# A sliding-window attention with a highway layer: loads of the first blocks by another queue and in another layout, a first batch pair by query blocks, and the highway layer in pairs of token blocks

## The chip, the cores and the metric

The kernel runs on one core of a Trainium2 chip. The metric is the device time of one execution in microseconds. Five engines work side by side, each on its own queue of instructions in order: TensorE (PE, with its weight loads PEld), VectorE (DVE), ScalarE (ACT), GpSimd (POOL) and SyncE (SP). GpSimd and SyncE also issue the DMAs here.

## The reference, cut to what matters

```python
B, H, S, D = 8, 8, 576, 64
scores = q @ k.T / 8                        # per batch and head
rel = pos[:, None] - pos[None, :]
mask = (rel >= 0) & (rel < 128)             # 128 keys back at most
scores = where(mask, scores - slopes[h] * abs(rel), -1e9)
attn = softmax(scores)
x = concat_heads(attn @ v)                  # 4608 tokens x 512
H_ = maximum(x @ w_h, 0)
T_ = 1 / (1 + exp(-(x @ w_t + b_t)))
out = T_ * H_ + (1 - T_) * x                # fp32
```

## The kernel before, in words

**Tiling.** Two batches form a pair m (0 to 3); the two lie on the two halves of the 128 rows (64 dimensions each) when scores are computed. The 576 tokens are blocks 0 to 3 of 128 and a narrow block 4 of 64 (the tail, both batches together on 128 rows). A block of queries sees its own block of keys and the one before it.

**Loads.** GpSimd casts fp32 to bf16 while loading. `load_qk` (L98) brings q or k in pieces of four tokens (1 KB read in one piece); for pair 0 the first half of the rows comes in eight loads of four heads and one batch, the second half in two. `load_v` (L123) brings one block of v in pieces of one token and head (256 B read), `load_tails` (L115) the narrow block. w_h is loaded by SyncE in fp32 into the room of q of pair 1 and cast by ScalarE (L221, L227); w_t and the bias come by GpSimd (L230).

**Attention.** TensorE transposes q and k (L251), DVE or ACT copies them out of PSUM (L277). Keys and queries of a load in pieces of four stand in a permuted order, which the copies of k undo and the masks for q take up. Per head: scores (L304), exp on ACT with the key's part of the slope as bias (L337), the mask as a product on DVE for two heads (L352), the product with v that has a column of ones (L375, matmuls at L393), and the division by the sum (L399, L409 and L410) into x. A pair is worked in stages, which `STAGES` and `ORDER` (L43, L51) set: pair 0 in four of 256 columns (a to d: blocks of keys 0, 1, 2, 3), the others in two of 512 (A, B).

**Highway layer**, per block of 128 tokens (36 in all, each a group of its own, `GROUPS`, L56): four transposes of x (L433), a copy (L442), four matmuls with w_h (L449), relu less x on DVE (L456), four matmuls with w_t (L465) and one that adds the bias by a one-hot row (L467), tanh on ACT (L473), the step from tanh to the gate on GpSimd (L478; on DVE in the last blocks), gate product on DVE (L483), addition of x on GpSimd (L489; the last on DVE), and the store by SyncE in four DMAs (L505), two for a tail (L497).

**Order.** A planner's output is written out: `ISSUE` (L714) lists the nodes in the order in which they are issued, `BANKS` (L750) the PSUM bank of each tile (eight banks; a score tile or a product with v of four or more blocks takes two). Each engine runs its instructions in that order. The nodes (L592 to L709) name their dependences; the costs and due times beside them are the planner's input and have no effect when the kernel runs. Pools (L65) bound how many tiles are alive.

Of the kernel before, what the change touches and what calls it, by code (L numbers as in the profile page):

```python
# [10 lines left out]
P = 128  # L11
# [3 lines left out]
def kernel(  # L15
# [30 lines left out]
        "a": ((0, 0, 0), (0, 1, 128)),  # L46
        "b": ((1, 1, 0), (1, 2, 128)),
        "c": ((2, 2, 0), (2, 3, 128)),
        "d": ((3, 3, 0), (3, 4, 128), (4, 4, 192)),
    }  # L50
    ORDER = ("abcd", "AB", "AB", "AB")  # L51
    DMA_X = ()

    HOME = {"A": ("A", 0), "B": ("B", 0), "a": ("A", 0), "b": ("A", 256), "c": ("B", 0), "d": ("B", 256)}

    GROUPS = {  # L56
        "A": ((0,), (1,), (2,), (3,)), "B": ((0,), (1,), (2,), (3,), (4,)),
        "a": ((0,), (1,)), "b": ((0,), (1,)), "c": ((0,), (1,)), "d": ((0,), (1,), (2,)),
    }

    ADD_MASK = ()
# [36 lines left out]
    def load_qk(m, w, x=None, hs=None):  # L98
        src, dst = ((q, QL), (k, KL))[w]
        ps = slice(0, P) if x is None else slice(64 * x, 64 * x + 64)  # L100
        for r in (slice(0, 2),) if hs is None else (0, 1):
            hh = slice(0, H) if hs is None else slice(4 * hs, 4 * hs + 4)
            if hs is None:
                o = dst[m % 2][ps].rearrange("p r h n -> p (r h) n")
                i = src[2 * m : 2 * m + 2, :, 4 * ps.start : 4 * ps.stop, :].rearrange(
                    "r h (p t) d -> p (r h) (t d)", t=4
                )
            else:
                o = dst[m % 2][ps, r, hh, :]
                i = src[2 * m + r, hh, 4 * ps.start : 4 * ps.stop, :].rearrange(  # L110
                    "h (p t) d -> p h (t d)", t=4
                )
            nc.gpsimd.dma_start(out=o, in_=i)  # L113
# [22 lines left out]
    MKA = ADD_MASK and cp.tile([P, H, 2 * P], BF16, name="mka")  # L136
    cvec = cp.tile([P, H], F32, name="cvec")
    ones1 = cp.tile([P, P], BF16, name="ones1")
    wH = cp.tile([P, NCK, DM], BF16, name="wH")
# [25 lines left out]


    BIG = float(2**20)

    def c_mka():
        nc.vector.tensor_scalar(out=MKA[:, :, 0:P], in0=bc(tri[:, 0, :], P), scalar1=BIG,  # L170
                                scalar2=-BIG, op0=ALU.mult, op1=ALU.add)
        for h in range(H):
            nc.vector.tensor_scalar(
                out=MKA[:, h, P : 2 * P], in0=tri[:, 1, :], scalar1=BIG,
                scalar2=-BIG - P * slopes[h] / scale, op0=ALU.mult, op1=ALU.add,
            )

# [13 lines left out]
    def c_vec():  # L191
        nc.vector.memset(ones1[:], 0.0)
        nc.vector.memset(ones1[0:1, :], 1.0)
        nc.vector.memset(bT[:], 0.0)
        for h in range(H):
            nc.vector.memset(cvec[:, h : h + 1], float(np.exp(-float(P) * slopes[h])))
# [20 lines left out]

    def w_stage():
        return QL[1][:].rearrange("p r h n -> p (r h n)").bitcast(F32)

    def load_wf():  # L221
        nc.sync.dma_start(
            out=w_stage().rearrange("p (c n) -> p c n", c=NCK),
            in_=moe_w_h.rearrange("(c p) n -> p c n", p=P),
        )

    def cast_wf():  # L227
        nc.scalar.copy(out=wH[:].rearrange("p c n -> p (c n)"), in_=w_stage())

    def load_w(n):  # L230
        if n == 2:
            nc.gpsimd.dma_start(out=bT[0:1, :], in_=moe_b_t.rearrange("(o n) -> o n", o=1))
        else:
            nc.gpsimd.dma_start(
                out=(wH, wT)[n][:],
                in_=(moe_w_h, moe_w_t)[n].rearrange("(c p) n -> p c n", p=P),
            )
# [5 lines left out]
    def chunks(m):  # L243
        return (0, 1) if ORDER[m][0] == "a" else (None,)

    def tr_parts(m):

        ps = [(x, hs) for x in chunks(m) for hs in range(4 if x is None else 2)]
        return ps + ["tail"]

    def transposes(m, w, part):  # L251
# [11 lines left out]
        x, hs = part  # L263
        L = (QL, KL)[w][i]
# [12 lines left out]
    def evac(m, w, part):  # L277
# [7 lines left out]
        x, hs = part  # L285
        nh, n0, n = (2, 0, P) if x is None else (4, 64 * x, 64)
# [14 lines left out]
    def width(kind):  # L301
        return 512 if kind in "AB" else 256

    def scores(m, kind, h):  # L304
        i, W = m % 2, width(kind)
        if W == 512 or h % 2 == 0:
# [3 lines left out]
        sc, o = SC[m, kind, h], 0 if W == 512 else (h % 2) * W  # L310
        qm = QT[i][:, h, 0:512].rearrange("p (t c q) -> p c t q", t=4, c=4)
        segs, n, add = STAGES[kind], 0, m == 0 and kind in ADD_MASK
        if add and h % 2 == 0:
            for r in range(2):
                nc.tensor.matmul(
                    out=sc[:, r, :], lhsT=ident[:],
                    rhs=MKA[:, h : h + 2, :].rearrange("p h n -> p (h n)"),
                    start=True, stop=False,
                )
        while n < len(segs):  # L320
            j, qb, off = segs[n]
            two = n + 1 < len(segs) and segs[n + 1][0] == j and segs[n + 1][1] < 4
            for r in range(2):
# [3 lines left out]
                else:  # L327
# [4 lines left out]
                    rhs=rhs, start=not add,  # L332
                    stop=not add or (h % 2 == 1 and n + 1 + two >= len(segs)),
# [3 lines left out]
    def soft(m, kind, h):  # L337
        W, (home, c0) = width(kind), HOME[kind]
        if h % 2 == 0:
            if c0 == 0:  # L340
                PT[m, home, h // 2] = ptp[home].tile([P, 2, 2, 512], BF16, name="pt")
            for j, qb, off in STAGES[kind]:
                COL[m, h // 2, j, qb] = (PT[m, home, h // 2], c0 + off)
        o = 0 if W == 512 else (h % 2) * W
        nc.scalar.activation(  # L345
            out=PT[m, home, h // 2][:, h % 2, :, c0 : c0 + W],
# [5 lines left out]
    def mask(m, kind, g):  # L352
        home, c0 = HOME[kind]
        o = PT[m, home, g]
# [3 lines left out]
        else:  # L358
            rep, lo, W = 2, c0, width(kind)
            if kind == "b":  # L360
                lo = 0
# [53 lines left out]

    def grp(m, kind, gi):
        bs = GROUPS[kind][gi]
# [9 lines left out]
    def f_x(m, kind, gi):  # L427
# [3 lines left out]
        for i in range(n):  # L431
            for c in range(NCK):
                nc.tensor.transpose(  # L433
                    out=pt[:, c * P : (c + 1) * P], in_=x[:, i, c * P : (c + 1) * P],
# [3 lines left out]
    def f_xe(m, kind, gi):  # L438
# [4 lines left out]
            out=xt[:, 0:n].rearrange("p i c n -> p i (c n)"), in_=TR[m, kind, gi][:, 0:512].rearrange("p (i n) -> p i n", i=1)  # L443
        )

    def f_h(m, kind, gi, i):
        AH[m, kind, gi] = ps_tile(1)
        for c in range(NCK):
            nc.tensor.matmul(out=AH[m, kind, gi], lhsT=XT[m, kind, gi][:, i, c, :],  # L449
                             rhs=wH[:, c, :], start=c == 0, stop=c == NCK - 1)  # L450

    def f_u(m, kind, gi):
# [4 lines left out]
            out=uu[:, 0:n, :], in0=AH[m, kind, gi].rearrange("p (i n) -> p i n", i=1), scalar=0.0, in1=x,  # L457
            op0=ALU.max, op1=ALU.subtract,
        )

    def f_z(m, kind, gi, i):
        AZ[m, kind, gi] = ps_tile(1)
        az = AZ[m, kind, gi]
        for c in range(NCK):
            nc.tensor.matmul(out=az, lhsT=XT[m, kind, gi][:, i, c, :], rhs=wT[:, c, :],  # L465
                             start=c == 0, stop=False)
        nc.tensor.matmul(out=az, lhsT=ones1[:], rhs=bT[:], start=False, stop=True)  # L467

    def f_th(m, kind, gi):
# [3 lines left out]
        nc.scalar.activation(out=tt[:, 0:n, :], in_=AZ[m, kind, gi].rearrange("p (i n) -> p i n", i=1), func=ACTF.Tanh,  # L473
# [11 lines left out]
    def f_out(m, kind, gi, eng):  # L485
        bs, n, x = grp(m, kind, gi)
        ot = op.tile([P, 2, DM], F32, name="ot")
        OT[m, kind, gi] = ot
        eng.tensor_tensor(out=ot[:, 0:n, :], in0=UU.pop((m, kind, gi))[:, 0:n, :], in1=x, op=ALU.add)  # L489
# [302 lines left out]
```

The softmax here doesn't subtract the row's maximum and nothing guards it: scores larger than these inputs give would overflow.

## Time and profile before

| | |
|---|---|
| three runs | 175.17, 175.18, 175.36 us; median 175.18 |
| profiled execution | 175.22 us, of which the span 173.5 |
| granted TensorE clock | 0.987 |
| mean of one instruction | exp of 1024 columns 1119 ns, of 512 696; mask of 1024 753, of 2048 1454; relu less x 684; gate product 538; tanh 602; copy of x 589; POOL addition 1365 |
| largest waits of engines | POOL for the gate product 24.8 us, ACT for scores 13.2, ACT for the gate's matmuls 11.9, PE for k 7.9 |

A row of the page names line, engine, operation, out<-in and count, then busy time and mean of one instruction, then the engine's idle time before it and what ended that. A window row names the stretch, then busy time of PE, PEld, DVE, ACT and POOL. The chain is followed back from the last instruction to what released each step. In the slices a digit is the busy share in tenths. A busy PE has matmuls in flight, which is not the same as full speed.

### The profile page before, as it was taken

How to read it: one execution, taken by the hardware profiler on the slowest of the kernel's cores; microseconds unless marked ns; L12 is line 12 of the kernel's file. 1: busy time of each engine (PE TensorE's matmuls, PEld its weight loads, DVE VectorE, ACT ScalarE, POOL GpSimd, SP SyncE). 2: the span in 40 equal slices, each digit the busy share in tenths (PEclk: the TensorE clock that was granted, in tenths of full speed). 3: DMA queues.
4: the chain of work that ended last, by engine and by line, in shares of the span. 5: the costliest groups of instructions: out<-in, count | busy, mean ns of one | idle time of the engine just before them, and what ended most of it. 6: DMA issues, size and time to landing. Idle time of an engine off the chain costs nothing.

```text
span 173.5 us, 5255 instructions
## 1 busy us (share of the span) xinstructions
PE 150.3 (87%) x2132; PEld 92.8 (54%) x2132; DVE 140.0 (81%) x244; ACT 125.4 (72%) x178; POOL 118.1 (68%) x132
## 2 busy tenths in 40 slices
PE   0169789999799789999999979999999999999930
PEld 0158544666566347766556755566556556754410
DVE  5087686999898888999867999889887899976580
ACT  2625678797799969899779968799898897235510
POOL 7997373488883799984067985884485969676540
PEclk9999999999999999999999999999999999999995
DMA  4999999999999999999999996793124332454443
GB/s 161 211 191 191 154 197 185 184 176 102 190 205 202 197 108 158 216 217 210 252 118 154 153 179 97 88 135 99 45 64 121 76 90 68 107 127 113 125 121 91
DMA packets 70167, 25.50 MB, mean 147 GB/s; under 512 B 48128, under 2 KB 65024, under 8 KB 70144
## 3 DMA queue, kind: packets, MB, share of 16 engines
q0 software_dynamic: 62832, 14.68, 120.7%
q1 hardware_dynamic: 7312, 10.49, 22.6%
q8 instruction: 16, 0.26, 0.7%
q14 instruction: 7, 0.06, 0.1%
HBM read 30.41 MB, written 9.44 MB: 230 GB/s over the span
## 4 chain that ended last, share of the span: by engine, by line
PE 53%; DMA 29%; DVE 5%; POOL 4%; ACT 3%; issue 2%; SPq 0%; POOLq 0%; ACTq 0%; DVEq 0%
DMA va<-in_v_dram 17%; PE ps L465 14%; PE ps L449 14%; DMA ktl<-in_k_dram 8%; PE ps L393 7%; PE ps L329 7%; PE ps L271 4%; PE ps L433 4%; DMA kl<-in_k_dram 3%; PE ps L467 3%; ACT pt L345 2%; DVE pt L364 1%; POOL kl L113 1%; DVE uu L456 1%; DMA out_dram<-ot 1%
## 5 line engine op out<-in xcount | busy, mean ns | idle before, releaser
L345 ACT ACTIVATE pt<-ps,bias 128x1024 bf16<-128x1024 f32 (+1 forms) x80 | 72.2, 950 | 13.5 <-PE ps L329 13.2
L489 POOL TENSOR_TENSOR ot<-uu,x 128x512 f32<-128x512 bf16 x35 | 47.7, 1365 | 24.9 <-DVE uu L483 24.8
L364 DVE TENSOR_TENSOR pt<-pt,mk 128x2048 bf16<-128x2048 bf16 (+1 forms) x40 | 46.5, 1174 | 0.8 <-ACT pt L345 0.8
L465 PE MATMUL ps<-wT,xt 128*128 128x512 bf16 x144 | 37.0, 379 | 1.0 <-DVE uu L456 0.8
L449 PE MATMUL ps<-wH,xt 128*128 128x512 bf16 x144 | 37.0, 386 | 0.3 <-DVE qt L290 0.3
L473 ACT ACTIVATE tt<-ps 128x512 f16<-128x512 f32 x36 | 21.6, 602 | 13.0 <-PE ps L467 11.9
L456 DVE SCALAR_TENSOR_TENSOR uu<-ps,x 128x512 bf16<-128x512 f32 x36 | 24.5, 684 | 4.6 <-PE ps L449 4.3
L329 PE MATMUL ps<-qt,kt 64*128 64x256 bf16 (+2 forms) x384 | 24.8, 248 | 3.4 <-DVE qt L290 1.1
L478 POOL TENSOR_SCALAR tt<-tt 128x512 f16<-128x512 f16 x32 | 21.8, 687 | 7.7 <-ACT tt L473 7.5
L410 DVE TENSOR_TENSOR x<-ps,rd 128x256 bf16<-128x256 f32 (+3 forms) x40 | 25.5, 638 | 1.4
L125 POOL DMA_DIRECT2D va<-in_v_dram x20 | 22.3, 1115 | 5.6 <-DMA ql<-in_q_dram 4.2
L393 PE MATMUL ps<-va,pt 128*128 128x65 bf16 (+1 forms) x576 | 24.9, 197 | 0.8 <-DMA va<-in_v_dram 0.7
L393 PEld LDWEIGHTS <-pt 128*128 128x128 bf16 (+1 forms) x576 | 21.1, 101 | 8.2 <-issue 2.9
L442 ACT COPY xt<-ps 128x512 bf16<-128x512 bf16 x36 | 20.7, 589 | 5.3 <-PE ps L433 5.1
L483 DVE TENSOR_TENSOR uu<-uu,tt 128x512 bf16<-128x512 bf16 x36 | 19.1, 538 | 4.3 <-POOL tt L478 4.1
L449 PEld LDWEIGHTS <-xt 128*128 128x128 bf16 x144 | 13.0, 99 | 14.3 <-issue 2.1
L465 PEld LDWEIGHTS <-xt 128*128 128x128 bf16 x144 | 12.9, 98 | 13.6 <-issue 1.5
L329 PEld LDWEIGHTS <-kt 64*128 64x128 bf16 x384 | 13.2, 96 | 12.9 <-issue 8.9
L271 PE MATMUL ps<-ident,kl 128*64 128x128 bf16 (+1 forms) x320 | 12.3, 228 | 8.1 <-DMA kl<-in_k_dram 7.9
L296 ACT COPY kt<-ps 128x1024 bf16<-128x1024 bf16 x13 | 13.0, 1020 | 5.4 <-PE ps L271 5.4
L271 PEld LDWEIGHTS <-kl 128*64 128x64 bf16 (+1 forms) x320 | 9.9, 126 | 10.1 <-DMA kl<-in_k_dram 8.4
L290 DVE COPY qt<-ps 128x1024 bf16<-128x1024 bf16 x16 | 11.0, 686 | 3.8 <-PE ps L271 3.7
(44 smaller groups left out, 125.5 us busy)
## 6 DMA issues: line engine op xcount, KB each, us to landing
out_dram<-ot SPq DMA_DIRECT2D x128, 64.0 KB, 2.4
va<-in_v_dram POOLq DMA_DIRECT2D x16, 256.0 KB, 14.2
ql<-in_q_dram POOLq DMA_DIRECT2D x3, 1024.0 KB, 16.0
kl<-in_k_dram POOLq DMA_DIRECT2D x3, 1024.0 KB, 15.7
ql<-in_moe_w_h_dram SPq DMA_DIRECT2D x1, 1024.0 KB, 5.2
out_dram<-ot SPq DMA_DIRECT2D x8, 128.0 KB, 2.4
kl<-in_k_dram POOLq DMA_DIRECT2D x4, 128.0 KB, 5.5
ql<-in_q_dram POOLq DMA_DIRECT2D x4, 128.0 KB, 5.9
```

What stands on the lines that cost most here:

```text
L125: nc.gpsimd.dma_start(out=VA[m % 2][0:n, c, :, :, 0:D].rearrange("s r h d -> s (r h) d"), in_=v[2 * m : 2 * m + 2, :, c * P : c * P + n, : ...
L271: nc.tensor.transpose(out=pt[r * D : (r + 1) * D, c : c + n], in_=L[ps, r, nh * hs + hl, t * D : (t + 1) * D], identity=ident[ps, ps],)
L329: nc.tensor.matmul(out=sc[:, r, o + off : o + off + w_], lhsT=KT[i][rows, h, j * P : (j + 1) * P], rhs=rhs, start=not add, stop=not add or ...
L345: nc.scalar.activation(out=PT[m, home, h // 2][:, h % 2, :, c0 : c0 + W], in_=SC[m, kind, h][:, :, o : o + W], func=ACTF.Exp, bias=BIAS[:, ...
L364: nc.vector.tensor_tensor(out=o, in0=o, in1=mk.to_broadcast([P, 2, rep, W]), op=ALU.mult,)
L393: nc.tensor.matmul(out=av[rows, hl, n * (D + 1) : (n + 1) * (D + 1)], lhsT=pt[:, hl, r, off : off + (D if narrow else P)], rhs=va[:, j, r, ...
L410: nc.vector.tensor_tensor(out=x.rearrange("p b (h d) -> p h b d", h=2), in0=av[:, :, :, 0:D], in1=rd[:, :, 0:nb].to_broadcast([P, 2, nb, D ...
L449: nc.tensor.matmul(out=AH[m, kind, gi], lhsT=XT[m, kind, gi][:, i, c, :], rhs=wH[:, c, :], start=c == 0, stop=c == NCK - 1)
L456: nc.vector.scalar_tensor_tensor(out=uu[:, 0:n, :], in0=AH[m, kind, gi].rearrange("p (i n) -> p i n", i=1), scalar=0.0, in1=x, op0=ALU.max ...
L465: nc.tensor.matmul(out=az, lhsT=XT[m, kind, gi][:, i, c, :], rhs=wT[:, c, :], start=c == 0, stop=False)
L478: eng.tensor_scalar(out=tt, in0=tt, scalar1=0.5, scalar2=0.5, op0=ALU.mult, op1=ALU.add)
L489: eng.tensor_tensor(out=ot[:, 0:n, :], in0=UU.pop((m, kind, gi))[:, 0:n, :], in1=x, op=ALU.add)
```

## The change

It has five parts.

1. Blocks 0 and 1 of q and k of pair 0 are loaded in natural order, one token and head a piece (256 B read). Their bf16 copies lie in the room of k of pair 1. The first four heads of block 0 come by SyncE in fp32 into the room of q of pair 1 and are cast by DVE (q) and ACT (k); the others come by GpSimd. Blocks 2 and 3 come as two loads. A transpose then takes 128 x 128 at once.
2. w_h comes by GpSimd with a cast, behind two blocks of v; w_t stands behind k of pair 1.
3. Pair 0 is worked in four stages by query blocks (e: block 0; f: block 1 with keys 1 and 0; g: block 2 with keys 2 and 1; h: the rest), of 128, 256, 256 and 384 columns.
4. The highway layer runs on groups of two blocks (14 groups), and singly for the narrow blocks and all of the last stage. For a group, copy, relu less x, tanh, gate step and gate product are one instruction of twice the size; the bias is set first by two matmuls of 64 rows each (L493 of the changed kernel), one per block; the additions stay single; a store is four DMAs for both blocks.
5. The last block's gate, products and store run in two halves of 256 columns (four DMAs).

`ISSUE` and `BANKS` are new throughout. Dead code (the added mask) goes.

```diff
-        "a": ((0, 0, 0), (0, 1, 128)),
-        "b": ((1, 1, 0), (1, 2, 128)),
-        "c": ((2, 2, 0), (2, 3, 128)),
-        "d": ((3, 3, 0), (3, 4, 128), (4, 4, 192)),
+        "e": ((0, 0, 0),),
+        "f": ((1, 1, 0), (0, 1, 128)),
+        "g": ((2, 2, 0), (1, 2, 128)),
+        "h": ((2, 3, 0), (3, 3, 128), (3, 4, 256), (4, 4, 320)),
...
-        "A": ((0,), (1,), (2,), (3,)), "B": ((0,), (1,), (2,), (3,), (4,)),
+        "A": ((0, 1), (2, 3)), "B": ((0, 1), (2, 3), (4,)),
...
+    def load_nat(w, b, hs):
+        src = (q, k)[w]
+        hh = slice(0, H) if hs is None else slice(4 * hs, 4 * hs + 4)
+        for r in range(2):
+            nc.gpsimd.dma_start(
+                out=nat(w, b)[:, hh, r, :],
+                in_=src[r, hh, b * P : (b + 1) * P, :].rearrange("h s d -> s h d"),
+            )
...
+    def load_raw(w):
+        for r in range(2):
+            nc.sync.dma_start(
+                out=raw(w).rearrange("p (h r d) -> p h r d", h=4, r=2)[:, :, r, :],
+                in_=(q, k)[w][r, 0:4, 0:P, :].rearrange("h s d -> s h d"),
+            )
+
+    def cast_raw(w):
+        cp_ = (nc.vector.tensor_copy, nc.scalar.copy)[w]
+        cp_(out=nat(w, 0)[:, 0:4].rearrange("p h r d -> p (h r d)"), in_=raw(w))
...
+    def f_zb(m, kind, gi):
+        AZ[m, kind, gi] = ps_tile(2)
+        for i in range(2):
+            rows = slice(i * D, (i + 1) * D)
+            nc.tensor.matmul(out=AZ[m, kind, gi][:, i, :], lhsT=hot2[rows, :], rhs=bT[rows, :],
+                             start=True, stop=False)
...
+    def e_z(m, kind, gi, hf):
+        if hf == 0:
+            AZ[m, kind, gi] = ps_tile(1)
+        az = AZ[m, kind, gi][:, half(hf)]
+        for c in range(NCK):
+            nc.tensor.matmul(out=az, lhsT=XT[m, kind, gi][:, 0, c, :], rhs=wT[:, c, half(hf)],
                              start=c == 0, stop=False)
-        nc.tensor.matmul(out=az, lhsT=ones1[:], rhs=bT[:], start=False, stop=True)
+        nc.tensor.matmul(out=az, lhsT=ones1[:], rhs=bT[:, half(hf)], start=False, stop=True)
...
+    def e_st(m, kind, gi, hf, eng):
+        for r in range(2):
+            row = (2 * m + r) * S + 512
+            eng.dma_start(out=out[row : row + D, half(hf)],
+                          in_=OT[m, kind, gi][r * D : (r + 1) * D, 0, half(hf)])
...
         if m == 0:
-            qk(0, 0)
-            qk(0, 1)
-            vv(0, 1)
-            for n_ in (1, 2):
+            nt(0, 0)
+            nt(0, 1)
+            vv(0)
+            nt(1, None)
+            vv(1)
+            for n_ in (0, 1, 2):
...
             qk(1)
             vv(2, 3)
             tl()
```

The issue order decides what goes first. On PE it is: transposes of k of block 0 (raw heads), of blocks 2-3 of k, of q of block 1, of k of block 0-1 and q of block 0, and then the scores of e and f. GpSimd's loads go: k of blocks 2-3; q of block 0 (upper heads); q of block 1; k of block 1; q of blocks 2-3; k of block 0 (upper heads); tails; two blocks of v; w_h; the bias; a block of v; k of pair 1; w_t; tails; q of pair 1; the rest of v.

## The prediction

> **What bounds the kernel now.** I read the page first (busy shares, the slices, the chain by line), then the windows of 10 us, then the chain in order of time, then the last 10 us of the timeline.
>
> ```profile
> PE 150.3 (87%) x2132; PEld 92.8 (54%) x2132; DVE 140.0 (81%) x244; ACT 125.4 (72%) x178; POOL 118.1 (68%) x132
> DMA  4999999999999999999999996793124332454443
> q0 software_dynamic: 62832, 14.68, 120.7%
> ```
>
> No engine is full over the span, and DMA is full for its first 60%. The windows split that:
>
> ```profile
> 20.00:30.00 10.00, 9.14 (x97) 4.88 (x92) 8.01 (x18) 6.86 (x13) 5.50 (x6) 1.00 1.74 186
> 70.00:80.00 10.00, 9.98 (x209) 7.31 (x208) 9.80 (x15) 8.98 (x12) 8.77 (x11) 1.00 1.66 211
> 120.00:130.00 10.00, 9.77 (x92) 5.57 (x89) 8.72 (x14) 8.97 (x14) 5.70 (x5) 1.00 0.27 66
> ```
>
> The columns are PE, PEld, DVE, ACT, POOL busy, clock, DMA share, GB/s. At 20-30 ACT and DVE are idle a fifth to a third of the time while DMA is full; from 120 on DMA is nearly idle and PE is always in flight. The chain agrees:
>
> ```profile
> 2.15 5.95 DMA kl<-in_k_dram
> 11.81 11.31 DMA va<-in_v_dram
> 26.31 17.49 DMA va<-in_v_dram
> 44.09 13.60 DMA ktl<-in_k_dram
> 58.22 0.97 PE ps L449 x4
> ```
>
> Up to 57.7 us the chain is the one GpSimd queue, each load landing 6 to 17 us after its issue; from there it is matmuls. The end:
>
> ```profile
> 158.99 10.17 SPq L505 DMA_DIRECT2D out_dram<-ot  x20
> 166.25 1.15 POOL L489 TENSOR_TENSOR ot<-uu,x 128x512 f32<-128x512 bf16 x1 [0.74 <-DVE uu L483]
> 169.25 1.11 SPq L497 DMA_DIRECT2D out_dram<-ot  x2
> ```
>
> Matmuls end at 166.2, but the span at 173.5: the last stores queue on SP, and the last block's (ready at 168.74) leave only after the four before them.
>
> So there are three regimes: loads (0-58), a mix of PE and DVE with loads just in time (58-95), PE (95-166), and a tail of 7 us.
>
> [...]the eight first loads (256 KB read each) landed 0.67 us apart, but the first at 6.72, behind w_h's 1 MB from SP.[...] Here a v chunk (0.5 MB in 256 B pieces) lands about 2.05 us after the one before, while a q or k load (2 MB in 1 KB pieces) takes 5.0 to 5.6: per byte three halves dearer.[...] four score matmuls of 64 rows x 256 columns are over in 0.39 us, against 0.216 for one of 512 columns alone.[...]
>
> **The change, part by part.** The sum is against the profiled execution: 175.22, span 173.5, so 1.7 lie around it; the median of three is 175.18.
>
> *Loads.* What GpSimd and SP must move before the second pair of batches can run: before, q and k of pair 0 in 1 KB pieces (4 MB, 10.7 us), w_h 2.7, five v chunks 9.2, tails 1.4, w_t 2.7, q and k of pair 1 10.8, tails 1.4 = 38.8. After, half of q and k of pair 0 (blocks 0 and 1) comes in 256 B pieces, as v does: 0.5 MB takes 2.05 instead of 1.33, four times, +2.9 us. So I put the complete set at 46.6 (landing of the last k tail of pair 1 in the trace) + 2.9 = 49.5.
>
> In the new order, from the effective start (12.21, landing of the eighth quarter, less 8 x 0.67, less 2.67 for w_h: 4.2): raw q, k 2.05 to 6.2; k of blocks 2-3 2.67 to 8.9; q of block 0, upper heads to 9.9; q of block 1 to 12.0; k of block 1 to 14.0; q of blocks 2-3 to 16.7; k of block 0, upper heads to 17.7; tails to 19.1; two v chunks to 23.2; w_h to 25.9; v to 27.9; k of pair 1 to 33.3; w_t to 36.0; tails; q of pair 1 to 42.8, or some 45.5 with what the same sum missed before (43 against 46.6).
>
> *First scores.* The raw heads land near 6, are cast (about 0.5 each, bounded by 0.42 and 0.69, DVE copies of 512 and 1024) and are transposed at once. But PE's order puts the transposes of k of block 1 ahead of every score, so the first score waits for 14.0: about 14.6 against 13.01 before, first exp about 15.0 against 14.15. The SP path buys nothing there, and its waits hold up nothing else: PE, ACT and DVE behind the casts would wait for 12.0 and 14.0 anyway. What comes back: the exps then run in one stretch (e 8 x 0.45, f 8 x 0.70 = 9.2), where before they came in fours with 1.2 us gaps (14.15, 17.75, 21.47). Counted in full heads (1024 columns), exps done by 25 us: before 6.0, after about 6; by 35: 10.5 against 12.5.
>
> *Later in pair 0.* w_t lands at 36.0 (25.8 before), so the first gates come at 37-38 instead of 30; and the last four heads of stage h are queued on PE behind q of pair 1 (45.5). By 45: 15 heads and 4 blocks before, 13 and 4 after. By 55, when exps of pair 1 flow: 19 and 4 before, 19 and 5 or 6 after. So the start is worth 0, from -1.5 (a block or so of FFN ahead at 1.9 us of PE, hidden in part) to +3 (the +2.9 uncovered). GpSimd's k load of pair 1 now waits for the transposes of blocks 0 and 1 (done by 18); w_t, tails and q of pair 1 stand behind it, and GpSimd issues a load only once the eighth before it has landed, so it reaches that load near 23: nothing. But eight of the smaller loads (0.5 to 1 us each) are only 5 to 7 us of work in flight; unfilled time of the queue there is part of C.
>
> *Transposes of pair 0*: 128 of 64x64 (0.033 each, 32 in 1.06) give way to 32 of 128x128 (0.056): -4.2 + 1.8 = -2.4 of PE, in the stretch where PE waits for loads: 0. *w_h's cast* (ACT 1.90, at 6.1) goes: ACT was idle to 11.95: 0.
>
> *Paired FFN* (28 of 36 blocks become 14 pairs). PE: the bias took 36 x 0.216 = 7.8; now 8 x 0.216 and 14 pairs of half-height matmuls side by side, 0.216 each: 4.8. That is -3.0, less the mode changes around them (a score's neighbour of full height starts 0.1 later than its own kind; six or seven more in the instruction order): -2.4; bounds -3.0 and, if the two ran in turn, +0.6. About 10 of the 14 pairs lie after 58 us, where PE counts: -1.7. DVE: [...]the gate product 2 x 0.538 become about 0.75 (the mask of 1024 bf16 columns, 0.753): -0.33. Together 14 x 0.5 = -7, of 140. ACT: copy 2 x 0.589 become 1.02, tanh 2 x 0.602 become 1.03: 14 x 0.33 = -4.6. GpSimd: 0.687 x 2 become about 1.2: -2. PE from 95 on doesn't gain by that; in 58-95, where DVE is at 9.8 of 10 in 70-80, I count a fifth of DVE's -4 there and after: -0.8. Against it: a pair's halves wait for each other and hold two banks twice as long[...], with scores taking two of the eight. Unknown; -0 to +3, taken as +0.3.
>
> *Stores.* A pair is four DMAs instead of eight: SP has room, but isn't late before 159 anyway: 0.
>
> *Tail.* The last block is computed in halves; its result comes about 1 us earlier, but SP isn't free: as before, the four stores of the block before it end 5.1 us after that block's gate matmuls. Then four stores instead of two: 2 x 0.42 = +0.8.
>
> Sum: 0 - 1.7 - 0.8 + 0.3 + 0.8 = -1.4 with the start at nil; with half a block to one block gained at the start (-0.9) -2.3: **172.9**.
>
> **Rivals.**
> - A, forecast: PE's saving and a little of DVE's, 172.9; own range 171 to 174.6. For: 120-160 is PE. Chance 0.40.
> - B, DVE was the true limit. DVE is at 8 to 9.8 of 10 from 30 to 160; if its -7 is worth two thirds (-4.7), with PE's -1.7 and the tail's +0.8, the sum is -5.6: 169.6. For: the waits of PE on DVE are short but everywhere. Against: nearly no idle time of PE is put down to DVE after 60. Chance 0.14.
> - C, slower: loads. The extra 2.9 us lie on the only queue in its full stretch, and w_t and q of pair 1 come late; if PE has no other work in 36-46 the 2.9 pass through to 58 and on, and pairs in eight banks leave 1 to 2 us of stalls. 175.2 + 2.9 + 1.5 + 0.8 - 2.4 = 178.0. It decides if fewer than 19 heads of exp are done at 55 us. For: the chain to 57.7 is this queue. Against: q and k of pair 3 land at 79 to 90 and are transposed at 93, with FFN work to run meanwhile. Chance 0.36.
> - D, nothing: the queue's loss and the tail eat PE's saving: 175.2. Chance 0.10.
>
> **Numbers.** Within 0.2% (0.35 us) is what a measurement can't tell from no change. Faster is A and B less A's slow edge: 0.53; same 0.09; slower 0.38. The range takes in B's and C's centres: 169.3 to 178.3.
>
> **What would show it.** First exp at 15 (before 14.15) and one stretch of exps behind it; q of pair 1 landing near 45; first gate matmul near 37; 19 heads and 5 to 6 blocks at 55; DVE's busy time near 133; the two half-height bias matmuls starting within some ns of each other; SP's last four issues after the POOL addition of the last but one block. It is wrong if first scores run by 10, if DVE's idle time grows in 60-120 by more than its saving, or if PE waits for a bank in most pairs.

## The result, and the profile after

The changed kernel takes 183.72 us (median of four runs, 182.07 to 184.80) against 175.18 (174.88 to 175.36): ratio 1.0481, 95% interval 1.0397 to 1.0565. It is 8.5 us slower, where 2.3 less were forecast. Run once more beside the experiments it took 182.82, ratio 1.0389 (1.0334 to 1.0444). Medians here and below are of all runs, while a ratio leaves out a kernel's runs that lie more than 1.5% above its fastest, so the two don't always convert into each other.

The profiled execution took 183.28 us, span 181.6. First the page's busy shares, the granted clock and DMA by slices, then the same three windows as before.

```profile
PE 150.4 (83%) x2089; PEld 94.3 (52%) x2089; DVE 140.1 (77%) x223; ACT 122.7 (68%) x153; POOL 116.0 (64%) x120
PEclk9999999999999999999999999999699999999996
DMA  4999999999999999999999908538308444444652
```

```profile
20.00:30.00 10.00, 8.50 (x150) 7.58 (x148) 7.55 (x22) 8.28 (x14) 7.19 (x9) 1.00 1.76 183
70.00:80.00 10.00, 8.81 (x184) 6.72 (x185) 8.84 (x15) 8.09 (x10) 4.52 (x6) 1.00 1.33 251
120.00:130.00 10.00, 6.77 (x60) 3.37 (x59) 9.05 (x6) 5.54 (x7) 4.63 (x4) 0.84 0.72 105
```

DVE's busy time is what it was (140.1 against 140.0), and it issues fewer instructions. The last window is the odd one: PE is at 6.77 of 10 where it was at 9.77, the clock is at 0.84, and DVE is 9.05 busy with **six** instructions, where before 14 made 8.72. In the slices the clock drops once before the end, at the 29th.

The chain of work that ended last, by engine:

```profile
PE 59%; DVE 17%; ACT 8%; issue 7%; DMA 5%; SPq 0%; DVEq 0%; ACTq 0%; POOLq 0%
```

DVE has 17% of it (5% before). DMA has 5% (29% before), which probably means less than it seems: in the first 58 us the chain could go by loads or by the engines that they feed, and here it seems to take the other branch.

**Where the time went.** Counting exps (in heads of 1024 columns) and gated blocks (tanh done), both kernels are level at 55 us (19 heads, 4 blocks) and at 60 (23 and 6). At 80 the changed kernel has 32 heads and 9 blocks against 32 and 10; at 130 it has 53 and 18 against 56 and 21. So nothing is lost while loads bound it, and the loss comes between 60 and 130. Adding up the gaps between the starts of PE's matmuls beyond what each needs at full clock (0.216 us for 512 columns, the usual step from one start to the next in both traces; gaps over 0.45 us, from 55 us on) gives 3.8 us before and 10.2 after. The largest is 3.4 us, at 123.5. The timeline of the changed kernel there:

```profile
119.76 1.67 DVE L561 TENSOR_TENSOR uu<-uu,tt 128x1024 bf16<-128x1024 bf16 x1
120.86 3.79 POOL L567 TENSOR_TENSOR ot<-uu,x 128x512 f32<-128x512 bf16 x3
121.35 4.39 DVE L385 TENSOR_TENSOR pt<-pt,mk 128x2048 bf16<-128x2048 bf16 x1
125.67 2.34 DVE L483 SCALAR_TENSOR_TENSOR uu<-ps,x 128x1024 bf16<-128x1024 f32 x2
126.93 1.41 PE L414 MATMUL ps<-va,pt 128*128 128x65 bf16 x24 [3.23 <-DVE uu L483]
128.93 2.12 ACT L368 ACTIVATE pt<-ps,bias 128x1024 bf16<-128x1024 f32 x2 [4.01 <-PE ps L353]
```

Columns: start, duration, engine, line, operation; in brackets the idle time before it and who ended it. Read it backwards. PE's product with v waits 3.23 us for a max-subtract (L483), because that, as I read it, frees its PSUM bank. The two max-subtracts ran at once and at their usual length (2.34 for two); they are late because the mask (L385) stood ahead of them in DVE's order: the first starts at 125.67, the mask ends at 125.74. The mask took 4.39 us. Its usual length is 1.22 (18 of the 24 of its shape took 1.21 to 1.23). What is beside it is GpSimd with three additions in a row, to 124.65; the mask ends 1.08 us after them. The same reckoning fits another long mask: at 88.75 it took 3.40 us, GpSimd's two additions ended at 91.06, the mask at 92.15. So these two masks end about where they would if they had stood still for the whole row and then run for nearly their usual 1.22 us; I call that a standstill. It doesn't always take the whole row:

```profile
111.19 2.75 DVE L385 TENSOR_TENSOR pt<-pt,mk 128x2048 bf16<-128x2048 bf16 x1
111.69 1.16 POOL L567 TENSOR_TENSOR ot<-uu,x 128x512 f32<-128x512 bf16 x1
112.81 1.60 POOL L556 TENSOR_SCALAR tt<-tt 128x512 f16<-128x512 f16 x1
```

Here the mask ran after one addition (it ends 1.09 us after it), and the gate step behind that addition waited instead: 1.60 us, where 0.61 is usual. In the trace the 4.39 us count as busy time, not as waiting, and no view of waits shows them. After the gap at 123.5 the clock records show half clock from 126.8 to 130.2: 3.4 us at half speed are another 1.7, by my estimate.

Groups kept apart by shape, of the changed kernel and then of the kernel before (busy us, mean ns, idle time ahead):

```profile
L567 POOL TENSOR_TENSOR ot<-uu,x 128x512 f32<-128x512 bf16 x34 | 43.7, 1298 | 13.2 <-DVE uu L561 12.2 <-POOL ot L567 0.9
L385 DVE TENSOR_TENSOR pt<-pt,mk 128x2048 bf16<-128x2048 bf16 x24 | 38.7, 1622 | 3.4 <-ACT pt L368 3.4
L483 DVE SCALAR_TENSOR_TENSOR uu<-ps,x 128x1024 bf16<-128x1024 f32 x14 | 17.0, 1217 | 3.0 <-PE ps L476 3.0
L561 DVE TENSOR_TENSOR uu<-uu,tt 128x1024 bf16<-128x1024 bf16 x14 | 10.6, 758 | 4.1 <-POOL tt L556 4.0
```

```profile
L364 DVE TENSOR_TENSOR pt<-pt,mk 128x2048 bf16<-128x2048 bf16 x24 | 34.7, 1454 | 0.8 <-ACT pt L345 0.8
L483 DVE TENSOR_TENSOR uu<-uu,tt 128x512 bf16<-128x512 bf16 x36 | 19.1, 538 | 4.3 <-POOL tt L478 4.1
```

The masks are the same 24 instructions on the same data, and their mean went from 1454 to 1622 ns. Measured against the 1.22 us of an undisturbed one, that is some 6 us of standstill before and 10 after. With the narrower masks and the gate products it is some 11 before and 13 after, so the amount hardly grew. What grew is the single standstill: two masks over 2 us before, five after. The longest one before has two additions beside it, and PE's largest gap (1.3 us) comes behind it:

```profile
97.57 2.27 POOL L489 TENSOR_TENSOR ot<-uu,x 128x512 f32<-128x512 bf16 x2
97.79 3.15 DVE L364 TENSOR_TENSOR pt<-pt,mk 128x2048 bf16<-128x2048 bf16 x1
```

**Theories.** T1: a DVE instruction with two inputs in SBUF (masks, gate products) stands still while GpSimd reads SBUF; a pair puts GpSimd's additions back to back, so the standstill becomes long, and long ones reach PE through the in-order queue of DVE and the banks. That the reads and the two inputs decide it was my assumption. The trace of the changed kernel shows this much: the five masks that took 2.18 to 4.39 us instead of 1.22 all have additions beside them, and the one at 121.35 waited out three; gate products of one block, usually 0.41 to 0.43, reach 1.40; the 14 max-subtracts of pairs, with one input in PSUM, all took 1.21 to 1.23, though additions ran beside nine of them. T2: the order of the plan and the banks that a pair holds do it, GpSimd has no part. T3, added later: too few tiles for the max-subtract. The load theory (rival C of the prediction) has the count at 55 us against it.

### The profile page after: what moved, and what is told of

It reads as the page before. It is cut to its first block, busy times and chain, and to the rows that moved or that the text cites. A ratio compares the mean times of both kernels' runs of the same rounds, so it can differ in the third digit from the quotient of the medians.

```text
span 181.6 us, 5004 instructions
## 1 busy us (share of the span) xinstructions
PE 150.4 (83%) x2089; PEld 94.3 (52%) x2089; DVE 140.1 (77%) x223; ACT 122.7 (68%) x153; POOL 116.0 (64%) x120
## 4 chain that ended last, share of the span: by engine, by line
PE 59%; DVE 17%; ACT 8%; issue 7%; DMA 5%; SPq 0%; DVEq 0%; ACTq 0%; POOLq 0%
PE ps L502 15%; PE ps L476 14%; PE ps L353 8%; PE ps L414 8%; PE ps L295 6%; DVE pt L385 5%; DMA kl<-in_k_dram 4%; DVE uu L483 4%; ACT pt L368 4%; PE ps L457 4%; DVE x L431 3%; ACT xt L467 2%; PE ps L282 2%; PE ps L493 2%; DVE uu L561 1%
## 5 line engine op out<-in xcount | busy, mean ns | idle before, releaser
L368 ACT ACTIVATE pt<-ps,bias 128x1024 bf16<-128x1024 f32 (+3 forms) x80 | 71.5, 950 | 19.5 <-PE ps L353 18.2
L385 DVE TENSOR_TENSOR pt<-pt,mk 128x2048 bf16<-128x2048 bf16 (+3 forms) x40 | 50.7, 1277 | 6.5 <-ACT pt L368 6.3
L556 POOL TENSOR_SCALAR tt<-tt 128x1024 f16<-128x1024 f16 (+1 forms) x19 | 20.1, 1061 | 27.9 <-ACT tt L551 27.9
L551 ACT ACTIVATE tt<-ps 128x1024 f16<-128x1024 f32 (+1 forms) x21 | 18.6, 884 | 15.6 <-PE ps L502 10.1
L353 PE MATMUL ps<-qt,kt 64*128 64x128 bf16 (+2 forms) x432 | 26.7, 247 | 2.6 <-DVE x L431 1.5
L483 DVE SCALAR_TENSOR_TENSOR uu<-ps,x 128x1024 bf16<-128x1024 f32 (+1 forms) x22 | 22.4, 1024 | 5.4 <-PE ps L476 5.4
L467 ACT COPY xt<-ps 128x1024 bf16<-128x1024 bf16 (+1 forms) x22 | 18.5, 863 | 2.1 <-PE ps L457 2.1
L561 DVE TENSOR_TENSOR uu<-uu,tt 128x1024 bf16<-128x1024 bf16 (+1 forms) x21 | 14.4, 692 | 5.5 <-POOL tt L556 5.4
L430 DVE RECIPROCAL rd<-ps 128x4 f32<-128x4 f32 (+3 forms) x40 | 7.9, 198 | 7.2 <-PE ps L414 7.1
L457 PE MATMUL ps<-ident,x 128*128 128x128 bf16 x144 | 11.6, 224 | 0.1
(64 smaller groups left out, 126.8 us busy)
```

The costliest lines, as they stand in the source:

```text
L353: nc.tensor.matmul(out=sc[:, r, o + off : o + off + w_], lhsT=KT[i][rows, h, j * P : (j + 1) * P], rhs=rhs, start=True, stop=True,)
L368: nc.scalar.activation(out=PT[m, home, no, h // 2][:, h % 2, :, c0 : c0 + W], in_=SC[m, kind, h][:, :, o : o + W], func=ACTF.Exp, bias=BIA ...
L385: nc.vector.tensor_tensor(out=o, in0=o, in1=mk.to_broadcast([P, 2, rep, W]), op=ALU.mult,)
L467: nc.scalar.copy(out=xt[:, 0:n].rearrange("p i c n -> p i (c n)"), in_=TR[m, kind, gi][:, 0 : 512 * n].rearrange("p (i n) -> p i n", i=n))
L483: nc.vector.scalar_tensor_tensor(out=uu[:, 0:n, :], in0=AH[m, kind, gi], scalar=0.0, in1=x, op0=ALU.max, op1=ALU.subtract,)
```

## The experiments

Times are medians; ratios are to the kernel before, measured beside each run. The unedited kernel ran once more, since the first runs of experiments 2 and 3 spread so widely:

> The changed kernel once more, unedited, so that the runs of this call have it beside them on the same chip. In the first call two kernels that differ from it by one instruction's place or by two stores had runs near 180.3 and runs near 184.8. If that is its own doing, it shows both groups here: some runs at 181 to 182, some at 184 to 185; if not, all runs lie within 182 to 185 as before.

Its six runs: 181.61, 182.18, 182.20, 183.45, 186.00 and 186.72. Near relatives of it (runs 2, 3 and 5, and one in 9) come out between 1.028 and 1.051, and their edits don't explain that spread. All of them lose 5 us or more to the kernel before; differences of 1 or 2 us between them say little.

**1. Additions without reads, in both kernels.** Each of GpSimd's additions adds its first 8 columns alone and fills the others with zeros. Waits and order are the same:

```diff
-        eng.tensor_tensor(out=OT[m, kind, gi][:, i, :], in0=UU[m, kind, gi][:, i, :],
-                          in1=x[:, i, :], op=ALU.add)
+        c = 8 if eng is nc.gpsimd else DM
+        eng.tensor_tensor(out=OT[m, kind, gi][:, i, 0:c], in0=UU[m, kind, gi][:, i, 0:c],
+                          in1=x[:, i, 0:c], op=ALU.add)
+        if c < DM:
+            eng.memset(OT[m, kind, gi][:, i, c:DM], 0.0)
```

> The changed kernel with GpSimd's additions cut down: each adds only its first 8 columns and fills the other 504 of its output with zeros, so the output lacks most of x + gated product; waits, order and DVE's work stay as they are. T1 (a DVE operation with two SBUF inputs stands still while GpSimd reads SBUF, and pairs put GpSimd's reads back to back): the masks of 2048 elements come down from a mean of 1.62 us to about 1.3, none near 4.4, PE's gap of 3.4 us at 123 and the half clock behind it vanish, time 175 to 178 (183.7 less 5 to 8). T2 (the order and the banks held by pairs, GpSimd has no part in it): masks and gap stay, time 181 or more.

> The control: the kernel before with the same cut in its GpSimd additions (output lacks the same part). T1: it loses little to the sharing as it is (mask mean 1.45, excess of all masks some 6 us, nearly no idle time of PE behind it), so 173.5 to 175.2. If it gains as much as the changed kernel does (5 or more), the additions are simply a cost in both and the comparison says nothing on the change.

Changed kernel: 175.20, ratio 0.9978 (0.9956 to 1.0000). Kernel before: 172.84, ratio 0.9871 (0.9818 to 0.9923). PE's gaps fall from 10.2 to 2.8 us, the clock stays full, and DVE's busy time is 128.3 (129.1 in the kernel before with the same cut). So what GpSimd does beside DVE costs the kernel before 2.6 us, somewhat more than T1 gave, and the changed kernel 7 to 9, depending on which of its two measurements is taken: T1. GpSimd is also 16 us less busy here, so this run alone doesn't separate what its additions read from how long they take; run 6 keeps all of them and moves only when they run. Masks in the changed kernel then:

```profile
L385 DVE TENSOR_TENSOR pt<-pt,mk 128x2048 bf16<-128x2048 bf16 x24 | 30.5, 1282 | 3.2 <-ACT pt L368 3.2
```

**2. The max-subtract ahead of the long mask.**

```diff
+    order.remove(("u", (2, "A", 0)))
+    order.insert(order.index(("msk", (2, "B", 3))), ("u", (2, "A", 0)))
```

> The changed kernel with one DVE instruction moved: the max-subtract of the pair of blocks that frees two banks at 126.9 us goes ahead of the mask that took 4.39 us. T2 (order): PE's gap of 3.4 us and the half clock go, time 178 to 179.5. T1: the mask still ends when GpSimd's three additions end, near 125.7, and the product with v needs the mask, so the gap shrinks by 1.2 us only, the clock drop may stay; time 181 to 183.

184.51 (180.11 to 185.44), ratio 1.0283 (1.0209 to 1.0357). In the profiled run (180.11) the mask still takes 3.25 us at 121.75; PE's gap is 2.1 us instead of 3.4 and the clock stays full. The gap shrank by the 1.2 us that T1 gave; the times don't tell the two apart, since the lowest, 180.11 and 180.47, lie between both figures. The order decides how a standstill is passed on, not whether there is one.

**3. The last block stored whole.**

```diff
-        for r in range(2):
+        for r in range(2) if hf else ():
             row = (2 * m + r) * S + 512
-            eng.dma_start(out=out[row : row + D, half(hf)],
-                          in_=OT[m, kind, gi][r * D : (r + 1) * D, 0, half(hf)])
+            eng.dma_start(out=out[row : row + D, :],
+                          in_=OT[m, kind, gi][r * D : (r + 1) * D, 0, :])
```

> The changed kernel with the last block stored by two DMAs of full width behind its second half instead of four of half width. Prediction's tail term (+0.8 from two more issues of 0.42 on SP, queued behind the block before it): 0.8 to 1.0 less, 182.7 to 182.9. If the four issues lie in the shadow of something else: no change, 183.7. The spread of this kernel between runs (182.1 to 184.8) may hide it; then the distance from PE's last end to the end of the span, 8.5 us, is to come down to 7.4 to 7.7.

180.60 (179.84 to 185.18), ratio 1.0287 (1.0236 to 1.0339): 1.8 us under the unedited kernel's 1.0389, more than the edit was to give, but run 2, with its tail as it was, came out as low. So the time doesn't show the tail's part. The distance from PE's last matmul to the end of the span does show it: 8.3 us in the changed kernel, 7.7 here, 7.3 before. (The expectation's 8.5 counted from the start of that matmul.) SyncE's last issues, of the changed kernel and of this one:

```profile
161.82 14.77 SPq L584 DMA_DIRECT2D out_dram<-ot  x24
176.69 2.39 SPq L544 DMA_DIRECT2D out_dram<-ot  x4
```

```profile
174.81 1.11 SPq L544 DMA_DIRECT2D out_dram<-ot  x2
```

**4. Each pair's instructions in two of 512.** Max-subtract, tanh, gate step and gate product are split; the first half goes one place forward in its engine's order where its block is ready, and so does the first addition.

```diff
+    def p_u(kb, i):
+        x = grp(*kb)[2]
+        if i == 0:
+            UU[kb] = ft.tile([P, 2, DM], BF16, name="uu")
+        nc.vector.scalar_tensor_tensor(
+            out=UU[kb][:, i, :], in0=AH[kb][:, i, :], scalar=0.0, in1=x[:, i, :],
+            op0=ALU.max, op1=ALU.subtract,
+        )
...
+        if key[0] in SPLIT and len(grp_n(*kb)) == 2:
+            seq5 += [(key, 0), (key, 1)]
...
+        if prev > src:
+            seq5.insert(prev, seq5.pop(at))
```

> The changed kernel with each pair's max-subtract, tanh, gate step and gate product issued as two instructions of 512 instead of one of 1024, each as early as its own block allows by one place in its engine's order, and the additions likewise; matmuls, bias pairs, loads and stores stay. T1 (GpSimd's reads back to back): the gate steps and additions are still bunched but in smaller pieces with gaps that let a mask in, 177 to 181. If the longer instructions are no trouble and only the planner's order is: 183 to 186, as DVE gets 14 x 0.27 us more work (2 x 0.686 + 2 x 0.56 - 1.217 - 0.758 = 0.52 by the trace of the changed kernel at most, 7 us in all). If pairing as such was the loss (banks held until both halves are done): 176 to 178.

186.75, ratio 1.0572 (1.0513 to 1.0630): slower than the pairs, so my figure for T1 missed. The standstill didn't go: one gate product took 3.22 us (0.41 undisturbed), and masks and gate products stood some 15 us in all. So halving the pair's instructions doesn't help, and pairs are not worse than two singles in nearly the same order.

**5. The first heads by GpSimd.** The raw copy and the casts go; GpSimd loads them with the cast.

```diff
-            nc.sync.dma_start(
-                out=raw(w).rearrange("p (h r d) -> p h r d", h=4, r=2)[:, :, r, :],
+            nc.gpsimd.dma_start(
+                out=nat(w, 0)[:, 0:4, r, :],
...
-        cp_ = (nc.vector.tensor_copy, nc.scalar.copy)[w]
-        cp_(out=nat(w, 0)[:, 0:4].rearrange("p h r d -> p (h r d)"), in_=raw(w))
+        pass
```

> The changed kernel with the first four heads of q and k of block 0 loaded by GpSimd with the cast in the transfer, and without the fp32 copy and the two casts. Prediction: the SP path buys nothing, because PE's order puts k of block 1 ahead of the first score, and the four small issues on GpSimd come first in its queue: 183 to 185, no sure difference (four more issues of some 0.76 us on GpSimd, 0 to +2). Load theory (the start is what costs): more than 3 us difference either way.

184.16 (182.78 to 185.08), ratio 1.0506 (1.0456 to 1.0556), against 1.0389 (1.0334 to 1.0444) for the unedited kernel beside it and 1.0481 when it was first measured: 2.0 us longer or 0.4, about what the four more issues on GpSimd would give. In its trace the first exp comes at 17.41 instead of 15.56, and 16 heads are done at 55 us instead of 19; at 130 it is 53 in both. Three heads lost at the start are made up for later, so the start is not the loss.

**6. All the work kept, additions behind masks.** The run that settles it. DVE writes a column after the mask that stands ahead of an addition in the order; GpSimd copies that column before it adds.

```diff
+        if key[0] == "msk" and key[1][1] in "AB":
+            lastm = key
+        elif key[0] == "o" and nodes[key][0] == "POOL" and lastm:
+            GATE[key] = MARK[lastm] = len(MARK)
+            lastm = None
...
+            if key in GATE:
+                j = GATE[key]
+                nc.gpsimd.tensor_copy(out=gs[:, 64 + j : 65 + j], in_=gs[:, j : j + 1])
             nodes[key][3]()
+            if key in MARK:
+                nc.vector.memset(gs[:, MARK[key] : MARK[key] + 1], 0.0)
```

> The changed kernel, all its work kept, with 15 or so of GpSimd's additions made to wait for a mask: DVE writes one column after the mask that stands ahead of the addition in the order, and GpSimd copies that column before it adds (about 0.1 us of DVE and 0.2 of GpSimd each). T1: the long masks are those that started while additions were running; now the mask runs first and the additions after it: masks at 88, 97, 111 and 121 us back to about 1.3, time 176 to 179. T2: GpSimd's work has no part in it: 183.5 to 186, the added waits only cost. If the additions then meet the next mask instead: 181 to 184, with long masks at other places.

175.62, ratio 1.0019 (0.9993 to 1.0046), beside 182.82 for the unedited kernel: a little under T1's 176 to 179. Instructions were added, order and banks stayed, and 7 us came back; T2 falls. The same place in its timeline:

```profile
117.84 1.22 DVE L483 SCALAR_TENSOR_TENSOR uu<-ps,x 128x1024 bf16<-128x1024 f32 x1
117.99 0.18 POOL L883 COPY gs<-gs 128x1 f32<-128x1 f32 x1 [1.06 <-DVE gs L886]
118.14 3.37 POOL L567 TENSOR_TENSOR ot<-uu,x 128x512 f32<-128x512 bf16 x3
119.69 1.23 DVE L483 SCALAR_TENSOR_TENSOR uu<-ps,x 128x1024 bf16<-128x1024 f32 x1 [0.63 <-PE ps L476]
119.81 0.91 PE L414 MATMUL ps<-va,pt 128*128 128x65 bf16 x24
```

GpSimd waited 1.06 us for the mask. The same three additions then ran beside the two max-subtracts, which have one input in PSUM: these took 1.22 and 1.23 us, their usual length, and the additions 3.37 instead of 3.79. PE's product with v waits for nothing. Over the whole run:

```profile
PE 146.4 (85%) x2069; PEld 93.2 (54%) x2089; DVE 130.7 (76%) x237; ACT 122.6 (71%) x153; POOL 114.1 (66%) x134
PEclk9999999999999999999999999999999999999995
```

```profile
L385 DVE TENSOR_TENSOR pt<-pt,mk 128x2048 bf16<-128x2048 bf16 x24 | 30.9, 1299 | 3.2 <-ACT pt L368 3.2
```

**7. Both repairs, and the waits in the kernel before.** The edits of 6 and 3 together; and the edit of 6 alone in the old kernel.

> The changed kernel with both repairs: GpSimd's additions wait for the mask ahead of them, and the last block is stored by two DMAs of full width. If the two are independent: 175.6 - 0.8 = 174.8, at or just under the kernel before (175.1). If the tail is set by DVE's last additions instead: 175.6.

> The control for the added waits: the kernel before with GpSimd's additions made to wait for masks in the same way. T1: it had some 6 us of mask excess, nearly none of it in PE's gaps, and gained 2.6 us with the additions cut; the waits are worth a part of that: 173 to 175. If it gains 7 us as the changed kernel did, then the waits are a gain of their own and the loss isn't the change's. If it gains 0 to 2, the changed kernel with the same waits stays level or slower, and the change as such is worth nothing even without the collision.

Repaired: 175.19, ratio 0.9966 (0.9941 to 0.9991). Old kernel with waits: 175.91, ratio 1.0025 (1.0000 to 1.0050). The waits are no gain of their own (they even miss the 173 to 175 that T1 gave). In the old kernel they take away little standstill: DVE's busy time is 138.6 us there, against 140.0 without them, while in the changed kernel it fell from 140.1 to 130.7. From 1.0019 to 0.9966 the whole store is worth about 0.9 us, give or take 0.6 by the two intervals.

**8. The reverse: bunching in the kernel before.** Single blocks, GpSimd's order alone changed (SyncE's stores move with the additions). Tiles hold one block instead of two, and there are more of them, so that the additions held back don't run the others short of room.

```diff
+    adds = [key for key in order if key[0] == "o" and nodes[key][0] == "POOL"]
+    for a, b in zip(adds[0::2], adds[1::2]):
+        if order.index(("st", a[1])) < order.index(b):
+            order.remove(("st", a[1]))
+            order.insert(order.index(b) + 1, ("st", a[1]))
+        order.remove(a)
+        order.insert(order.index(b), a)
...
-        "pA": 5, "pB": 4, "x": 3, "xt": 5, "uu": 3, "tt": 3, "ot": 3,
+        "pA": 5, "pB": 4, "x": 4, "xt": 5, "uu": 5, "tt": 3, "ot": 4,
```

> The reverse: the kernel before, all single blocks, with GpSimd's order alone changed: of each two additions the first is held back until just ahead of the second (buffers for one block instead of two, so that there are more of them; all other engines' orders as they were). T1: two additions back to back are what hurts, so masks of 3 us and more appear and the time rises to 177 to 181. If bunching alone is no trouble and it takes the pair's other effects (banks, order): 175 to 176.

185.72, ratio 1.0547 (1.0490 to 1.0605). That is more than T1's 177 to 181. No pair, no new load, no new order on PE, DVE or ACT, and a loss as large as the change's is there. Its timeline:

```profile
119.58 2.27 POOL L489 TENSOR_TENSOR ot<-uu,x 128x512 f32<-128x512 bf16 x2
119.65 4.99 DVE L364 TENSOR_TENSOR pt<-pt,mk 128x2048 bf16<-128x2048 bf16 x1
121.83 0.61 POOL L478 TENSOR_SCALAR tt<-tt 128x512 f16<-128x512 f16 x1
122.42 1.14 POOL L489 TENSOR_TENSOR ot<-uu,x 128x512 f32<-128x512 bf16 x1
125.69 0.61 PE L329 MATMUL ps<-qt,kt 64*128 64x256 bf16 x8 [3.02 <-DVE x L410]
```

GpSimd's run ends at 123.56, the mask at 124.64: again 1.08 later. The gate step between the additions (0.61 us) didn't let the mask run either, so it belongs to the row.

**9. What is pairing worth, and is it a shortage of tiles?** The singles of 4 with both repairs; the same with four tiles instead of three; and the changed and the repaired kernel with four.

```diff
-        "pA": 5, "pB": 4, "x": 3, "xt": 5, "uu": 3, "tt": 3, "ot": 3,
+        "pA": 5, "pB": 4, "x": 3, "xt": 5, "uu": 4, "tt": 3, "ot": 3,
```

> What pairing itself is worth once the collision is out of the way: the kernel with both repairs (175.2), but with max-subtract, tanh, gate step and gate product of a pair issued as two instructions of 512 as in the run of singles. Prediction: pairing saves DVE 7 us of busy time, worth 0.8 of the span, so 176.0. If DVE is not late anywhere once nothing blocks it: 175.2. If the singles still lose to GpSimd, because the waits stand ahead of additions and gate steps are now twice as many: 178 or more, with gate products over 1 us.

> The run of singles with waits (184.5) with four buffers instead of three for the max-subtract's and tanh's tiles. In its trace DVE stands still for 2.5 us at 121.5 behind GpSimd's additions because the next max-subtract has no free tile, and PE waits 2.7 us for it. If that is its loss: the gap goes and the time falls to 177 to 180; what then still lies above 175.2 is what pairing saves. If the loss lies in gate products and masks that still meet additions (excess of 11 us in that trace): 182 or more.

> The changed kernel with four of these tiles instead of three and nothing else. T1: the tiles are not what DVE waits for (its long masks end 1.08 us after GpSimd's last addition, whatever the tiles), so 181 to 184, no sure difference. T3 (a shortage of tiles, because a pair's additions release a tile only after the second of them): 176 to 179.

> The kernel with both repairs (175.2) with four of these tiles. If some of its time is still max-subtracts waiting for a tile: 174 to 174.8. If not: 175.2.

Singles with waits: 184.46, ratio 1.0535 (1.0498 to 1.0572); four tiles: 179.67, ratio 1.0267 (1.0225 to 1.0309). The first has a wait that is shown as one:

```profile
121.69 3.36 POOL L567 TENSOR_TENSOR ot<-uu,x 128x512 f32<-128x512 bf16 x3
123.98 1.89 DVE L879 SCALAR_TENSOR_TENSOR uu<-ps,x 128x512 bf16<-128x512 f32 x3 [2.51 <-POOL ot L567]
125.32 0.94 PE L414 MATMUL ps<-va,pt 128*128 128x65 bf16 x16 [2.55 <-DVE uu L879]
```

With a fourth tile it is gone and about 5 us with it; masks and gate products still stand for some 12 us in that trace. My split takes the pair's tile earlier and puts gate products in new places, so these two runs don't say what pairing alone is worth; that stays open. The changed kernel with four tiles: 184.36, ratio 1.0454 (1.0388 to 1.0519), with the same mask of 4.39 us and PE's same gap of 3.4. T3 falls for it. The repaired kernel with four: 174.69, ratio 0.9973 (0.9949 to 0.9997), level with 0.9966. These two repaired kernels are the fastest that keep all the work, by 0.3%, some 0.5 us.

## Why the prediction was wrong, point by point

- *Start, taken as 0 with 0.9 of gain.* The 0 held: first exp at 15.56 (15.0 forecast), q of pair 1 landed at 43.55 (45), first gate matmul at 37.7 (37 to 38), 19 heads at 55. The raw heads landed between 3.2 and 9.3 instead of near 6, which was hidden: the last transposes ahead of the first score ran at 14.13, behind a copy of q by ACT. The half block to one block gained didn't come: 4 gated blocks at 55 in both. "The SP path buys nothing" was too strong: run 5, without it, starts its exps 1.85 us later, though that is worth 2.0 us of the time at most.
- *Bias pairs, part of PE's -1.7.* The two matmuls start 0 to 79 ns apart, as forecast, and each takes 0.37 to 0.39 us (0.63 in the one pair under half clock). The prediction's own sign of matmuls side by side, 0.39 us for four against 0.216 for one, set a record's whole length against the step from one start to the next; a single record of 512 columns is 0.38 long, so the four, over in 0.39, overlapped all the same. What the bias pairs saved of the time wasn't isolated; PE's busy time can't tell, since matmul records are missing from some traces.
- *DVE -7, worth -0.8.* Mis-sized, and a case to remember. Max-subtracts and gate products together went from 39.8 us to 35.7 where the additions are cut in both kernels (run 1): -4.1, not -7. The row I took for a single gate product, 0.538, was a mean that already held standstill; undisturbed it is 0.415. A pair takes 0.689 then, so it saves 0.14 and not 0.33. For the max-subtract the 0.5 of a pair leaves 0.17, an estimate that no trace showed; the pair's saves 0.15 (twice 0.684 less 1.217), a small matter.
- *"Against it: a pair's halves wait for each other and hold two banks twice as long ... taken as +0.3."* **This is the step that failed.** Its upper bound of 3 was too small, and its mechanism was not the one: pairs hold the same banks in run 6, where the loss is gone, and none in run 8, where it is there. In the same paragraph GpSimd was costed as an engine of its own ("0.687 x 2 become about 1.2: -2"; a pair's step usually takes 1.03 to 1.05). I never asked which DVE instruction runs beside it, although the kernel before had masks of up to 3.1 us in its trace where the rest take 1.22. What the runs put in its place: GpSimd's additions in a row, beside which masks (up to 4.39 us in the changed kernel and 4.99 in run 8, usually 1.22) and gate products (up to 1.67 and usually 0.68 to 0.69 for a pair in the changed kernel) stand still, +7 us (undone by run 6, made anew by run 8), including the half clock behind PE's gap at 123.5.
- *Tail +0.8.* About right: 0.9 (give or take 0.6) by runs 6 and 7, 0.6 by the traces of run 3.
- *Stores, and the waits of PE, ACT and DVE at the start: 0.* Nothing in the traces speaks against it. GpSimd's wait for the eighth load before shows in the trace of the kernel before: its 18th load goes at 19.21, after a wait of 2.69; the 10th had landed at 18.92.
- *Rival C* had the sign and not the reason. Its test was fewer than 19 heads at 55 us; there were 19. Run 5 has 16 and still loses only 0.4 to 2.0 us more.
- *Signs that would show it wrong.* I watched DVE's idle time and PE's waits for banks. Neither rose in the way described (DVE is idle for 6.4 us of the stretch from 60 to 120 in both kernels): standstill is counted as busy time. DVE's busy time near 133 was the useful sign: it came out at 140.1, and 130.7 once the collision was gone.

Without the collision the change brings no clear gain. With the waits in both kernels and the whole store it is ahead by 1.0 us (0.9966 against 1.0025), but there the old kernel keeps most of its standstill. With the additions cut in both, where little is left in either, it is behind by 1.9 us by the ratios and 2.4 by the medians, of which 0.9 is the tail. So apart from the collision, too, the sum of -2.3 was some 4 us too low. The gain at the start that didn't come (0.9) and the mis-sized DVE term are part of that; why PE's -1.7 doesn't show stays open.

The clock's part isn't measured by itself. In the changed kernel half clock comes at 126.81 for 3.41 us, when PE has been idle for some 3.1, and again at 178.01. The length of the idle time alone doesn't decide it: in the kernel before half clock comes at 168.88, 2.7 us after PE's last matmul, while in run 8 none follows the 3.02 us in which PE waits ahead of 125.69 (its slices stay at 9 there), nor run 2's gap of 2.1. What decides it isn't shown. Nor does the clock alone spread the run times: two runs of the changed kernel with the same mean clock of 0.974 took 182.07 and 184.80.

## What to carry to other kernels

Before you bunch work on GpSimd, list what DVE runs beside it: here masks and gate products, both inputs in SBUF, took up to 4.99 us (usually 1.22) and 3.22 (usually 0.41) beside rows of GpSimd's additions, and the profile calls that busy. Look for it as a spread within one group (same line, same shape, 1.22 and 4.39 us), and take an undisturbed duration, not the mean, for the cost of an instruction that you mean to merge. Where the work can't be moved, a wait that makes GpSimd start behind the long DVE instruction cost GpSimd 0.20 us on average in run 6, and the 14 of them brought back 7 us; in the kernel before they brought nothing.

## What the hardware showed unasked

- A mask can wait out a whole row of GpSimd's instructions: two additions (3.40 us), three (4.39) and a row of three additions and a gate step (4.99), each time ending about 1.08 us after the last of them. It isn't always shut out: at 111.19 in the changed kernel it ran after one addition, ahead of a gate step; at 108.63, 145.52 and 150.52 the mask took its usual 1.21 to 1.22 us beside an addition, which took 2.06 to 2.07 where 1.15 is usual.
- GpSimd's issuing of loads went with a longer DVE instruction too, but not each time: in the changed kernel a mask took 1.61 us at 57.90 with nothing but two issues beside it (57.53 to 59.83), and the next, at 59.77, 1.21 beside another (59.80 to 60.97). The gate product at 119.76 above took 1.67 instead of 0.68 beside an issue and the start of an addition. Why isn't shown.
- A max-subtract with one input in PSUM ran beside the same additions at its usual 1.22 us.
- GpSimd loses too, though less: its additions took 1.30 us on average in the changed kernel and 1.17 with the waits.
